# Layer 0's expert tiles 8 to 15 converted straight into weight slots, and the rows of s loaded together

## The chip, the cores and the metric

The kernel runs on one core of one Trainium2 chip. The time is that of the device for one execution, in microseconds; the median of several runs counts. The profile comes from one execution of its own, so its time differs a little from the median.

## The reference

Three stages follow each other, all in float32, on 4 batches, 8 heads, 576 positions, 512 model columns:

```
# attention, per batch and head
scores = (q @ k.T) / sqrt(64)
cum    = cumsum(maximum(s, 0))                       # s: (4, 8, 576)
scores = where(causal, -1e9, scores + minimum(-(cum[:, None] - cum[None, :]), 0))
attn   = softmax(scores);  x = attn @ v              # heads side by side: (4, 576, 512)
# layer 0
xn = (x - mean) / sqrt(var + 1e-6) * g_ln
x  = x + maximum(xn @ w_ch1, 0) @ w_ch2              # 512 -> 2048 -> 512
# layer 1: mixing over positions (U 576x32, V 32x576), then a second pair of 512 -> 2048 -> 512
u  = x + (x.T @ U @ V).T
out = u + maximum(u @ w_ch1', 0) @ w_ch2'
```

The weights arrive as float64 bit patterns and are turned into float32 on the chip.

## The kernel before, in words

**Tiles and steps.** The 2048 hidden columns are 16 tiles m of 128. Positions are cut into block A (the first 256) and block B (the other 320) of each batch. One *step* is one tile m on one block: `mlp1` multiplies by the tile's part of w_ch1, a relu follows, and `mlp2`, two steps later (`LAG`), multiplies by its part of w_ch2. Every product is done as three float32r matmuls on a high and a low part (lines 1364 to 1366 and 1397 to 1399). Layer 0 has 128 steps in this order: A0 and A1 (the block A of batches 0 and 1) on tiles 0 to 7 as steps 0 to 15, the same two on tiles 8 to 15 as steps 16 to 31, then A2 and A3 on tiles 8 to 15 and 0 to 7, then B0 to B3 one by one. Layer 1 has steps 128 to 207.

**Weight slots.** The pool `w` has 16 buffers of 512 KB: 8 tiles (`WSLOTS`), each with its half of w_ch1 (half 0) and of w_ch2 (half 1). When a later instance of a tile wants a slot, it takes that of the instance 8 before it, whose last use must be over. Tile n's first instance from 8 on has the slot of tile n - 8, which step n uses last.

**Conversion.** `f64_to_f32` takes a raw half tile (512 KB in a buffer of `wr`, of which there are four) with two ACT instructions (lines 517, 518) and one of DVE (line 520) into a PSUM bank; `split` then writes the high part (a copy on ACT or DVE, lines 374 or 375) and the low part (a subtraction on DVE, line 379).
- Tiles 0 to 7 (`fresh`) are split straight into their `w` slots (`w_split`) and the slot is also written to DRAM (`w_dr`, line 557), since later instances are read back from there (line 550).
- Tiles 8 to 15 go another way (`w_ahead`): raw load, conversion in place in `wr`, write to `w_dr` (line 566), and later a load into the slot. `W0` says over which steps these are laid.
- Layer 1's weights are converted ahead too (`w1_ahead`, `w2_ahead`), over the steps that `W1` gives.

**The front.** Before step 0, s is loaded. Four copies of its 32 rows stand on four groups of 32 partitions of `sc`, one load each, in two parts of columns (0 to 255, 256 to 575). relu and scaling (line 436), a running sum (line 438), its differences (line 451) and `ksum` (lines 457, 459) follow; the first matmul of the attention's scores reads `ksum` (line 761). A0's attention and its layer norm must be over before step 0.

**What sets the order.** Nothing is ordered by the program text. Each operation is given to a planner (`Plan`) with a priority, a cost, alternatives (ACT, DVE or POOL), and its reads and writes under keys; it places all of them on the engines by a list schedule, repeated `PASSES` times with due times from the schedule before. The emitted order of each engine, and of SP, which issues all DMAs, is the plan's. For the planner two operations that write the same key follow each other; the four row loads of one part have one key, `("s", c)`. Side work has positions in steps: `AT` (attention of each later block), `LN` (its layer norm), `W0`, `W1`. Where the plan leaves TensorE nothing to do before step 0, filler matmuls are put in (line 1552), which write a bank that nobody reads.

Of the kernel before, what the change touches and what calls it, by code (L numbers as in the profile page):

```python
# [31 lines left out]
LAST = ("C0", "C1", "C2", "C3", "T0")  # L32
W2SLOTS = 12

AT = {"A2": (3, 11), "A3": (6, 35), "B0": (24, 46), "B1": (48, 59), "B2": (67, 84), "B3": (78, 98)}
LN = {"A2": 15, "A3": 35, "B0": 59, "B1": 61, "B2": 84, "B3": 98}
W0 = (0, 8)
W1 = (10, 72, 50)
PASSES = 4


# [287 lines left out]
def mha_ffn_mixer_ffn(ctx: ExitStack, tc, qkv_p, qkv_a, qkv_b, s, g, w1, w2, U, V, out):  # L329
# [22 lines left out]
    def psum():  # L352
        return P.buf("ps", [128, 512])
# [15 lines left out]
    def load(prio, nbytes, fn, reads, writes, gate=None, rate=350.0):  # L369
        P.op(prio, {"sp": (475, fn)}, reads, writes, nbytes, gate, rate=rate)  # L370
# [13 lines left out]
    def split(prio, n, hi, lo, src, reads, wh, wl, psum=False, soft=0.0, slow=False):  # L384
        copy(prio, n, hi, src, reads, wh, psum, soft, slow)
        tt(prio, n, lo, src, lambda: f(hi()), ALU.subtract, list(reads) + list(wh), wl, psum, soft)
# [26 lines left out]
    def setup():  # L413
        sc, cum = P.buf("xc", [128, 1280]), P.buf("v", [128, 1280])
        late = 5
        part = ((0, 256, PRO), (256, S, late))

        for c, (c0, c1, pr) in enumerate(part):
            for y in range(4):
                load(pr, R * (c1 - c0) * 4, lambda y=y, c0=c0, c1=c1: nc.sync.dma_start(sc[R * y:R * (y + 1), c0:c1], s[:, c0:c1]), [], [(sc, ("s", c))])  # L420
        P.op(PRO, {"pool": (400, lambda: make_identity(nc, ident.tile))}, [], [ident])
        dve(PRO, 1, lambda: nc.vector.memset(eps.tile, 1e-6), [], [eps])
        dve(PRO, 1, lambda: nc.vector.memset(small.tile, 1e-9), [], [small])
        dve(PRO, 128, lambda: nc.vector.memset(ones.tile, 1.0 / DM), [], [ones], 0.521)
        P.op(PRO, {"pool": (600, lambda: nc.gpsimd.memset(causal.tile, 0.0))}, [], [causal])
        for y in range(4):
            act(PRO, R, lambda y=y: nc.scalar.activation(sel[R * y:R * (y + 1)], ident[R * y:R * (y + 1), R * y:R * (y + 1)], AF.Copy),
                [ident], [(sel, "y%d" % y)])

        def mask(d, n):  # L430
            return lambda: nc.gpsimd.affine_select(out=d, in_=d, compare_op=ALU.is_ge, fill=-8e9, base=0, pattern=[[-1, n]], channel_multiplier=1)

        P.op(PRO, {"pool": (266, mask(causal[:, 384:], 128))}, [causal], [causal])
        for c, (c0, c1, pr) in enumerate(part):
            k = (sc, ("s", c))
            dve(pr, c1 - c0, lambda c0=c0, c1=c1: nc.vector.tensor_scalar(out=sc[:, c0:c1], in0=sc[:, c0:c1], scalar1=0.0, scalar2=8.0, op0=ALU.max, op1=ALU.mult),
                [k], [k], 0.521)
            dve(pr, c1 - c0, lambda c0=c0, c1=c1: nc.vector.tensor_tensor_scan(
                cum[:, c0:c1], sc[:, c0:c1], sc[:, c0:c1], cum[:, c0 - 1:c0] if c0 else 0.0, ALU.add, ALU.max),
                [k] + [(cum, 0)] * c, [(cum, c)], 2.084)  # L440

        REL = {1: (sc, 576), 2: (sc, 832), 3: (sc, 0), 4: (cum, 640)}
        for i, (a, c) in REL.items():
            c0, c1 = COL[i], COL[i] + KEYS[i]
            pr = PRO if i == 1 else late
            key = [(a, ("s", y)) for y in range(2)] if i == 3 else [(a, 10 + i)]

            def rel(y0=0, y1=4, a=a, c=c, i=i):
                return a[R * y0:R * y1, c:c + KEYS[i]]

            dve(pr, KEYS[i], lambda i=i, rel=rel: nc.vector.tensor_scalar(
                out=rel(), in0=cum[:, :KEYS[i]], scalar1=cum[:, KEYS[i] - 1:KEYS[i]], scalar2=None, op0=ALU.subtract),
                [(cum, y) for y in range(1 + (i > 1))], key, 0.521, 128)
            if i == 4:
                load(pr, R * S * 4, lambda rel=rel: nc.sync.dma_start(cum_dr.tile, rel(0, 1)), key, [cum_dr])
                break
            act(pr, KEYS[i], lambda c0=c0, c1=c1, rel=rel: nc.scalar.activation(ksum[:, c0:c1], rel(), AF.Copy), key, [(ksum, i)])
            for y in (1, 3):
                dve(pr, KEYS[i], lambda y=y, c0=c0, c1=c1, rel=rel: nc.vector.tensor_tensor(
                    out=ksum[R * y:R * (y + 1), c0:c1], in0=rel(y, y + 1), in1=f(ksum[R * y:R * (y + 1), c0:c1]), op=ALU.subtract),  # L460
                    key + [(ksum, i)], [(ksum, i)])
        load(-1000, 2048, lambda: nc.sync.dma_start(g_sb.tile, g.rearrange("(k p) -> p k", p=128)), [], [g_sb])
        act(-1000, 4, lambda: nc.scalar.activation(g_sb.tile, g_sb.tile, AF.Copy, scale=-0.5), [g_sb], [g_sb])
# [38 lines left out]
    w_dr = {}  # L502
    for n, it in enumerate(inst):
        k = (it["l"], it["m"])
        it["fresh"] = k not in seen and n < WSLOTS
        if k not in seen:
            seen[k] = n
            w_dr[k] = P.fixed(dr_p.tile([128, 2, 2, 512], F32, name=f"w_dr{k[0]}_{k[1]}"))
    def f64_to_f32(prio, n, dst, raw, bd, br, words=(0, 1), psum=False):

        def pair(i):
            return raw().rearrange("p (c t) -> p c t", t=2)[:, :, i]

        def dv(fn, reads, writes):
            P.op(prio, {"dve": (68 + 1.042 * n, fn)}, reads, writes, port=not psum)

        act(prio, n, lambda: nc.scalar.activation(dst(), pair(1), AF.Prelu, scale=2.0 ** -112, alpha=-2.0 ** 32), [(br, words[1])], [bd], 135)
        act(prio, n, lambda: nc.scalar.activation(pair(0).bitcast(I32), pair(0).bitcast(U32), AF.Copy, scale=2.0 ** -29 * 0.9374),
            [(br, words[0])], [(br, words[0])], 135)
        dv(lambda: nc.vector.scalar_tensor_tensor(out=dst().bitcast(U32), in0=dst().bitcast(U32), scalar=3, in1=pair(0).bitcast(U32),  # L520
                                                  op0=ALU.logical_shift_left, op1=ALU.bitwise_or), [bd, (br, words[0])], [bd])

    def w_raw(prio, l, m, half, gate):
        raw = P.buf("wr", [128, 1024])

        def go():
            dst = raw.tile.bitcast(U32)
            if half == 0:
                nc.sync.dma_start(dst.rearrange("p (k c) -> p k c", k=KT), w1[l][m].bitcast(U32))
            else:  # L530
                nc.sync.dma_start(dst, w2[l][m * 128:(m + 1) * 128, :].bitcast(U32))

        load(prio, 128 * 4096, go, [], [raw], gate)
        return raw
# [8 lines left out]
    def w_split(n, half, gate):  # L543
# [11 lines left out]
        f64_to_f32(prio, 512, lambda: t.tile, lambda: raw.tile, t, raw, psum=True)  # L555
        split(prio, 512, lambda: w[:, 0], lambda: w[:, 1], lambda: t.tile, [t], [(w, 0)], [(w, 1)], psum=True)
        load(it["last"], 128 * 4096, lambda: nc.sync.dma_start(dr[:, half], f(w.tile)), [w], [(dr, half)])

    def w_ahead(n, half, gate):

        it = inst[n]
        prio, dr = it["first"] - 8, w_dr[it["l"], it["m"]]
        raw, t = w_raw(prio, it["l"], it["m"], half, gate), psum()
        f64_to_f32(prio, 512, lambda: t.tile, lambda: raw.tile, t, raw, psum=True)
        split(prio, 512, lambda: raw[:, :512].bitcast(F32R), lambda: raw[:, 512:].bitcast(F32R), lambda: t.tile, [t], [(raw, 0)], [(raw, 1)], psum=True)
        load(prio, 128 * 4096, lambda: nc.sync.dma_start(dr[:, half], raw.tile.rearrange("p (z c) -> p z c", z=2)), [raw], [(dr, half)])


    def w2_ahead(m, gate):
        prio = NS0 + m - 8  # L570
# [851 lines left out]
    def spread(items, a, b):  # L1422
        tot = sum(w for w, _ in items) or 1
        acc = 0.0
        for w, fn in items:
            put(a + (b - a - 0.25) * acc / tot, fn)
            acc += w

    halves = [(n, z) for n in range(len(inst)) for z in range(2)]

    def w_next(k, gate):
        if k < len(halves):
            w_load(*halves[k], gate)

    def w_step(k, gate):
        w_split(*halves[k], gate)
        w_next(k + 2, gate)

    for k, (n, z) in enumerate(halves):
        if n >= WSLOTS:  # L1440
            put(inst[n - WSLOTS]["last"] + LAG + 1 + 0.5 * z, lambda p, g, k=k: w_step(k, g))
    ahead = [(n, z) for n in range(WSLOTS, 2 * WSLOTS) for z in range(2)]
    for k, (n, z) in enumerate(ahead):
        if k >= 2:
            put(W0[0] + W0[1] * (k - 2) / 16, lambda p, g, n=n, z=z: w_ahead(n, z, g))
    for m in range(MT):
        at = W1[0] + W1[1] * m / 8 if m < 8 else W1[0] + W1[1] + W1[2] * (m - 8) / 8
        if m % 2 == 0:
# [76 lines left out]
    layer_norm_tok(4, 1)  # L1525
    for b in range(2):
        x_columns(10 + 8 * b, b)
    w_next(0, None)
    w_next(1, None)
    for k in range(2 * WSLOTS):  # L1530
        w_step(k, None)
    for n, z in ahead[:2]:
        w_ahead(n, z, None)

    def side(q):
        for pos, fn in plan.pop(q, []):
# [66 lines left out]
```

## Time and profile before

| | us |
|---|---|
| median of 3 runs | 1058.73 |
| lowest, highest | 1057.51, 1061.54 |
| the profiled execution | 1057.54 |
| its span | 1055.8 |
| granted TensorE clock, share of full speed | 0.999 |

PE is TensorE's matmuls, PEld its weight loads, DVE VectorE, ACT ScalarE, POOL GpSimd, SPq the DMA issues of SyncE. A line L550 is line 550 of the kernel. A matmul's busy time is modelled, and matmuls overlap each other; so sums of busy time by line can be longer than the stretch that they cover. Counts of records can be off by a few per cent. A wait is put down to what ended last.

### The profile page before, as it was taken

The page shows a single profiled execution, that of the slowest core. Times are in us where ns is not written, and L with a number is a line of the kernel's source. Part 1 is how long each engine was busy: PE and PEld are TensorE (multiplying, and loading weights), DVE is VectorE, ACT ScalarE, POOL GpSimd, SP SyncE. Part 2 cuts the span into 40 slices and gives each one's busy share as a digit, 9 for nine tenths or more (in the row PEclk, how much of TensorE's full clock was granted, in tenths as well). Part 3 has the DMA queues.
Part 4 walks back from the last instruction along what each step waited for, and adds up shares of the span by engine and source line. Part 5 has one row for each costly group of instructions (what it writes and reads, how often), then busy time and mean ns, then how long its engine had stood idle before and what let it go on. Part 6 is the DMA issues. An engine that isn't in the chain of part 4 may idle for free.

```text
span 1055.8 us, 20049 instructions
## 1 busy us (share of the span) xinstructions
PE 1038.2 (98%) x7469; PEld 967.0 (92%) x7469; DVE 676.2 (64%) x1709; ACT 490.1 (46%) x1152; POOL 150.8 (14%) x289
## 2 busy tenths in 40 slices
PE   9999999999999999999999999999999999999997
PEld 7799998899899999998999999898899999989997
DVE  6898777885897766787682526746455645744521
ACT  7978767774776566676552413412112211211211
POOL 0002123430541031323120001001000000100000
PEclk9999999999999999999999999999999999999999
DMA  9999999657833696487268799993663475276383
GB/s 310 343 325 347 365 325 308 189 164 283 269 126 133 235 351 202 136 291 269 68 232 331 241 337 367 341 365 116 222 232 135 135 268 186 94 259 206 121 279 100
DMA packets 100096, 253.55 MB, mean 240 GB/s; under 512 B 16512, under 2 KB 46464, under 8 KB 95648
## 3 DMA queue, kind: packets, MB, share of 16 engines
q1 hardware_dynamic: 100000, 252.28, 69.3%
q8 instruction: 59, 0.97, 0.4%
q14 instruction: 37, 0.30, 0.1%
HBM read 198.69 MB, written 62.99 MB: 248 GB/s over the span
## 4 chain that ended last, share of the span: by engine, by line
PE 78%; DVE 7%; DMA 6%; ACT 4%; issue 1%; SPq 0%; POOL 0%; DVEq 0%; ACTq 0%; POOLq 0%
PE ps L1364 6%; PE ps L1366 5%; PE ps L1365 5%; PE ps L1286 5%; PE ps L1288 5%; PE ps L1287 5%; PE acc L1397 4%; PE acc L1399 4%; PE acc L1398 4%; PE ps L862 3%; PE ps L820 3%; PE acc L1323 3%; PE acc L1324 3%; PE ps L1323 3%; PE ps L1324 3%; PE acc L1325 3%
## 5 line engine op out<-in xcount | busy, mean ns | idle before, releaser
L1364 PE MATMUL ps<-xh,w 128*128 128x256 f32 (+1 forms) x512 | 159.9, 312 | 1.0 <-DVE hl L1371 0.9
L1366 PE MATMUL ps<-xl,w 128*128 128x256 f32 (+1 forms) x512 | 151.3, 296 | 0.0
L1365 PE MATMUL ps<-xh,w 128*128 128x256 f32 (+1 forms) x512 | 151.3, 295 | 0.0
L1397 PE MATMUL acc<-hh,w 128*128 128x256 f32 (+1 forms) x448 | 136.2, 304 | 0.0
L1371 DVE SCALAR_TENSOR_TENSOR hl<-ps,hh 128x256 fp32r<-128x256 f32 (+1 forms) x144 | 64.7, 449 | 106.7 <-ACT hh L1370 105.7
L1399 PE MATMUL acc<-hl,w 128*128 128x256 f32 (+1 forms) x448 | 130.0, 290 | 0.1
L1398 PE MATMUL acc<-hh,w 128*128 128x256 f32 (+1 forms) x448 | 129.9, 290 | 0.0
L1370 ACT ACTIVATE hh<-ps 128x256 fp32r<-128x256 f32 (+1 forms) x144 | 58.0, 403 | 125.9 <-PE ps L1366 125.1
L1364 PEld LDWEIGHTS ps<-xh,w 128*128 128x128 f32 x512 | 97.0, 189 | 4.3 <-DVE hl L1371 1.1
L1365 PEld LDWEIGHTS ps<-xh,w 128*128 128x128 f32 x512 | 97.1, 190 | 0.6
L1246 ACT ACTIVATE w<-hl 128x256 fp32r<-128x256 f32 x88 | 36.0, 417 | 131.5 <-DVE hl L1266 131.5
L1366 PEld LDWEIGHTS ps<-xl,w 128*128 128x128 f32 x512 | 96.8, 189 | 0.0
L1397 PEld LDWEIGHTS acc<-hh,w 128*128 128x128 f32 x448 | 85.3, 190 | 3.5 <-issue 2.2
L1398 PEld LDWEIGHTS acc<-hh,w 128*128 128x128 f32 x448 | 85.3, 190 | 0.4
L1399 PEld LDWEIGHTS acc<-hl,w 128*128 128x128 f32 x448 | 85.1, 190 | 0.3 <-DVE hl L1371 0.3
L779 ACT ACTIVATE t<-t,mx 128x384 f32<-128x384 f32 (+4 forms) x112 | 68.9, 618 | 28.6 <-DVE mx L769 25.4
L1266 DVE TENSOR_TENSOR hl<-ps,hh 128x256 f32<-128x256 f32 x128 | 48.6, 419 | 47.9 <-PE ps L1288 46.8
L1266 DVE TENSOR_TENSOR hh<-ps,hh 128x256 f32<-128x256 f32 x64 | 27.1, 423 | 76.1 <-ACT hh L374 74.8
L379 DVE TENSOR_TENSOR pB<-ps,pB 128x512 fp32r<-128x512 f32 (+1 forms) x112 | 62.4, 571 | 16.3 <-ACT pB L374 15.6
L374 ACT ACTIVATE pB<-ps 128x512 fp32r<-128x512 f32 (+3 forms) x119 | 59.1, 502 | 25.5 <-PE ps L820 25.2
L820 PE MATMUL ps<-ident,t 128*128 128x128 f32 x400 | 64.8, 276 | 4.6 <-POOL wr L381 1.4
L374 ACT ACTIVATE hh<-ps 128x256 f32<-128x256 f32 x31 | 11.9, 384 | 109.7 <-PE ps L1288 109.6
(249 smaller groups left out, 2825.0 us busy)
## 6 DMA issues: line engine op xcount, KB each, us to landing
w<-w_dr SPq DMA_DIRECT2D x128, 512.0 KB, 7.5
pB<-w_dr SPq DMA_DIRECT2D x34, 1024.0 KB, 5.3
w_dr<-wr SPq DMA_DIRECT2D x48, 512.0 KB, 5.5
qk<-w_dr SPq DMA_DIRECT2D x26, 768.0 KB, 5.6
wr<-w1a SPq DMA_DIRECT2D x16, 512.0 KB, 5.9
wr<-w2a SPq DMA_DIRECT2D x16, 512.0 KB, 6.1
w_dr<-w SPq DMA_DIRECT2D x16, 512.0 KB, 6.8
wr<-w1b SPq DMA_DIRECT2D x16, 512.0 KB, 7.2
```

Of the source, the lines that this page charges most:

```text
L374: "act": ((51 if psum else 94) + 0.8333 * n, lambda: nc.scalar.activation(out(), a(), AF.Copy)),
L779: act(prio, K, lambda t=t, mx=mx, o=o, K=K, x=x, y=nt * z + x: nc.scalar.activation(t[:, o:o + K], t[:, o:o + K], AF.Exp, bias=mx[:, (1 if ...
L820: nc.tensor.transpose(ps[:, 128 * j:128 * (j + 1)], t[:, c:c + 128], ident.tile)
L1266: dve(st - 1000, 256, lambda: nc.vector.tensor_tensor(out=d.tile, in0=region(r), in1=a.tile, op=ALU.add), [p, a], [d])
L1323: nc.tensor.matmul(aa[z].tile, w[:, 0, sl], h[:, 0], start=first, stop=False)
L1364: nc.tensor.matmul(ps[:, :n], lhs(k, 0), xh[:, k, :n], start=k == 0, stop=False)
L1365: nc.tensor.matmul(ps[:, :n], lhs(k, 1), xh[:, k, :n], start=False, stop=False)
L1366: nc.tensor.matmul(ps[:, :n], lhs(k, 0), xl[:, k, :n], start=False, stop=k == KT - 1)
L1371: dve(st - 1000, n, lambda: nc.vector.scalar_tensor_tensor(out=hl[:, :n], in0=ps[:, :n], scalar=0.0, in1=f(hh[:, :n]), op0=ALU.max, op1=AL ...
L1397: nc.tensor.matmul(a, w[:, 0, sl], hh[:, :n], start=new, stop=False)
L1398: nc.tensor.matmul(a, w[:, 1, sl], hh[:, :n], start=False, stop=False)
L1399: nc.tensor.matmul(a, w[:, 0, sl], hl[:, :n], start=False, stop=last and (z == 1 or blk == "B"))
```

## The change

Five edits go together.
- The four row loads of s have a key of their own each, so that for the planner none of them follows another; those who read the rows name all four keys.
- Tiles 8 to 15 are `fresh` as well. `w_ahead` is gone. Their raw loads go through `w_next`, and `w_split` converts them straight into their `w` slots, laid one position behind the last use of the slot (instead of three for those that are read back); the slot is then written to DRAM as those of tiles 0 to 7 are.
- Raw loads are issued three half tiles ahead instead of two.
- `AT`, `LN` and `W1` have other values. `W0` has too, but nothing reads it any more.
- `it16` is only another name for the flag `fresh`.

```diff
-AT = {"A2": (3, 11), "A3": (6, 35), "B0": (24, 46), "B1": (48, 59), "B2": (67, 84), "B3": (78, 98)}
-LN = {"A2": 15, "A3": 35, "B0": 59, "B1": 61, "B2": 84, "B3": 98}
-W0 = (0, 8)
-W1 = (10, 72, 50)
+AT = {"A2": (1, 13), "A3": (1, 34), "B0": (28, 48), "B1": (48, 61), "B2": (67, 84), "B3": (78, 98)}
+LN = {"A2": 17, "A3": 34, "B0": 61, "B1": 61, "B2": 84, "B3": 98}
+W0 = (1, 14)
+W1 = (16, 66, 53)
...
-                load(pr, R * (c1 - c0) * 4, lambda y=y, c0=c0, c1=c1: nc.sync.dma_start(sc[R * y:R * (y + 1), c0:c1], s[:, c0:c1]), [], [(sc, ("s", c))])
+                load(pr, R * (c1 - c0) * 4, lambda y=y, c0=c0, c1=c1: nc.sync.dma_start(sc[R * y:R * (y + 1), c0:c1], s[:, c0:c1]), [], [(sc, ("s", c, y))])
...
-            k = (sc, ("s", c))
+            k = [(sc, ("s", c, y)) for y in range(4)]
...
-        it["fresh"] = k not in seen and n < WSLOTS
+        it["fresh"] = k not in seen
...
-    def w_ahead(n, half, gate):
-
-        it = inst[n]
-        prio, dr = it["first"] - 8, w_dr[it["l"], it["m"]]
-        raw, t = w_raw(prio, it["l"], it["m"], half, gate), psum()
-        f64_to_f32(prio, 512, lambda: t.tile, lambda: raw.tile, t, raw, psum=True)
-        split(prio, 512, lambda: raw[:, :512].bitcast(F32R), lambda: raw[:, 512:].bitcast(F32R), lambda: t.tile, [t], [(raw, 0)], [(raw, 1)], psum=True)
-        load(prio, 128 * 4096, lambda: nc.sync.dma_start(dr[:, half], raw.tile.rearrange("p (z c) -> p z c", z=2)), [raw], [(dr, half)])
...
     def w_step(k, gate):
         w_split(*halves[k], gate)
-        w_next(k + 2, gate)
+        w_next(k + 3, gate)
 
     for k, (n, z) in enumerate(halves):
         if n >= WSLOTS:
-            put(inst[n - WSLOTS]["last"] + LAG + 1 + 0.5 * z, lambda p, g, k=k: w_step(k, g))
-    ahead = [(n, z) for n in range(WSLOTS, 2 * WSLOTS) for z in range(2)]
-    for k, (n, z) in enumerate(ahead):
-        if k >= 2:
-            put(W0[0] + W0[1] * (k - 2) / 16, lambda p, g, n=n, z=z: w_ahead(n, z, g))
+            put(inst[n - WSLOTS]["last"] + (1.0 if it16(n) else LAG + 1) + 0.5 * z, lambda p, g, k=k: w_step(k, g))
...
-    w_next(0, None)
-    w_next(1, None)
+    for k in range(3):
+        w_next(k, None)
     for k in range(2 * WSLOTS):
         w_step(k, None)
-    for n, z in ahead[:2]:
-        w_ahead(n, z, None)
```

## Rows read from the trace of the kernel before

**Rows 1.** The page's head and part 1: busy time, share, instructions.

```profile
span 1055.8 us, 20049 instructions
PE 1038.2 (98%) x7469; PEld 967.0 (92%) x7469; DVE 676.2 (64%) x1709; ACT 490.1 (46%) x1152; POOL 150.8 (14%) x289
```

**Rows 2.** Windows: stretch, length, busy of each engine, clock, DMA share, GB/s.

```profile
0.00:22.10 22.10, 20.10 (x166) 17.08 (x166) 12.87 (x24) 15.41 (x29) 1.72 (x10) 1.00 0.90 315
22.10:51.20 29.10, 27.59 (x234) 21.81 (x235) 25.59 (x98) 27.40 (x65) 0.41 (x2) 1.00 0.95 334
51.20:82.00 30.80, 30.48 (x272) 29.12 (x271) 27.76 (x93) 24.91 (x68) 3.21 (x6) 1.00 0.96 326
...
82.00:149.00 67.00, 66.20 (x574) 63.76 (x573) 56.38 (x155) 49.50 (x140) 11.88 (x24) 1.00 0.99 355
...
51.20:560.00 508.80, 501.04 (x3857) 473.75 (x3856) 397.09 (x1021) 341.28 (x825) 127.73 (x262) 1.00 0.73 245
```

**Rows 3.** Windows of line 1552 (fillers): PE busy, PEld busy, clock, DMA.

```profile
0.00:22.10 22.10, 20.10 (x166) 17.08 (x166) 1.00 0.90 315
22.10:51.20 29.10, 5.74 (x39) 3.73 (x39) 1.00 0.95 334
```

**Rows 4.** Timeline of the front: start, length, engine, line, operation, what the wait ended.

```profile
0.75 0.40 SPq L420 DMA_DIRECT2D xc<-s  x1
...
12.43 0.42 SPq L420 DMA_DIRECT2D xc<-s  x1
...
18.70 0.29 DVE L436 TENSOR_SCALAR xc<-xc 128x256 f32<-128x256 f32 x1
...
22.14 0.78 PE L761 MATMUL ps<-ksum,sel 64*128 64x128 f32 x2 [0.91 <-DVE ksum L459]
...
51.25 0.36 PE L1364 MATMUL ps<-xh,w 128*128 128x256 f32 x1
```

**Rows 5.** Line 420, the eight row loads of s: time from issue to landing.

```profile
DMA to landing us min/median/max: 1.7/6.0/6.6
```

**Rows 6.** Groups by line, 0 to 51.2 us: busy, mean ns, idle before.

```profile
L520 DVE SCALAR_TENSOR_TENSOR ps<-ps,wr 128x512 uint32<-128x512 uint32 x15 | 10.4, 693 | 8.4 <-ACT wr L518 8.4
L379 DVE TENSOR_TENSOR w<-ps,w 128x512 fp32r<-128x512 f32 x15 | 10.2, 683 | 0.2
...
L518 ACT ACTIVATE wr<-wr 128x512 int32<-128x512 uint32 x17 | 11.3, 672 | 0.8 <-DMA wr<-w2a 0.7
L517 ACT ACTIVATE ps<-wr 128x512 f32<-128x512 f32 x16 | 10.2, 636 | 4.7 <-DMA wr<-w1a 4.6
...
L374 ACT ACTIVATE w<-ps 128x512 fp32r<-128x512 f32 x12 | 7.0, 591 | 0.6 <-DVE ps L520 0.6
```

**Rows 7.** Waits of ACT and DVE, 0 to 22.1 us: in total, times, longest.

```profile
ACT ps L517 <- DMA wr<-w1a: 4.6, 3, 1.9
...
DVE ps L520 <- ACT wr L518: 8.2, 5, 5.1
```

**Rows 8.** Windows of line 520 (one per conversion): DVE busy and count.

```profile
51.20:82.00 30.80, 4.13 (x6) 1.00 0.96 326
82.00:113.00 31.00, 5.46 (x8) 1.00 0.98 352
113.00:149.00 36.00, 2.06 (x3) 1.00 0.99 358
```

**Rows 9.** Window of line 1364 (four in each step): PE and PEld busy, counts.

```profile
51.20:82.00 30.80, 9.02 (x30) 5.70 (x30) 1.00 0.96 326
```

**Rows 10.** Waits of TensorE, 51.2 to 560 us, the four longest.

```profile
PE ps L820 <- POOL wr L381: 1.4, 1, 1.4
PE ps L962 <- DVE ls L379: 1.1, 1, 1.1
PE ps L820 <- DVE mx L748: 0.9, 1, 0.9
PE ps L1364 <- DVE hl L1371: 0.9, 1, 0.9
```

**Rows 11.** Instructions on w_dr: issue ns min/median/max, first and last start, count.

```profile
L550 SPq DMA_DIRECT2D w<-w_dr x96: 319/422/1725, 101.3 to 627.7; - x96
...
L566 SPq DMA_DIRECT2D w_dr<-wr x16: 319/374/806, 60.1 to 139.2; - x16
```

More of the change, by code (lines that the diff above doesn't have):

```diff
@@ L434, in setup @@
         for c, (c0, c1, pr) in enumerate(part):
-            k = (sc, ("s", c))
+            k = [(sc, ("s", c, y)) for y in range(4)]
             dve(pr, c1 - c0, lambda c0=c0, c1=c1: nc.vector.tensor_scalar(out=sc[:, c0:c1], in0=sc[:, c0:c1], scalar1=0.0, scalar2=8.0, op0=ALU.max, op1=ALU.mult),
-                [k], [k], 0.521)
+                k, k, 0.521)
             dve(pr, c1 - c0, lambda c0=c0, c1=c1: nc.vector.tensor_tensor_scan(
                 cum[:, c0:c1], sc[:, c0:c1], sc[:, c0:c1], cum[:, c0 - 1:c0] if c0 else 0.0, ALU.add, ALU.max),
-                [k] + [(cum, 0)] * c, [(cum, c)], 2.084)
+                k + [(cum, 0)] * c, [(cum, c)], 2.084)
         REL = {1: (sc, 576), 2: (sc, 832), 3: (sc, 0), 4: (cum, 640)}
@@ L445, in setup @@
             pr = PRO if i == 1 else late
-            key = [(a, ("s", y)) for y in range(2)] if i == 3 else [(a, 10 + i)]
+            key = [(a, ("s", c, y)) for c in range(2) for y in range(4)] if i == 3 else [(a, 10 + i)]
             def rel(y0=0, y1=4, a=a, c=c, i=i):
@@ L1427, in spread, with it16 @@
             acc += w
+    def it16(n):
+        return inst[n]["fresh"]
     halves = [(n, z) for n in range(len(inst)) for z in range(2)]
```

## The prediction

> **What bounds the kernel now.** I read the page first: TensorE (PE) is busy 1038.2 us of a span of 1055.8 [rows 1]. The reader should see there that little can be gained by feeding TensorE better on average, and ask where the missing time lies. The busy time by stretch answers it [rows 2]. From step 0 (the first expert matmul, at 51.25 us [rows 4]) to 560 us TensorE is idle 508.80 - 501.04 = 7.8 us in all, and its longest single wait there is 1.4 us [rows 10]. Ahead of step 0 it is different. The filler matmuls of line 1552, which compute nothing, fill 20.10 us of the first 22.1 us and 5.74 us of the next 29.1 [rows 3]. TensorE is idle 22.10 - 20.10 = 2.0 us and 29.10 - 27.59 = 1.5 us there. Of the 51.2 us ahead of step 0, then, 20.10 + 5.74 + 2.0 + 1.5 = 29.3 us do no work and 21.9 us do. That front is the only large loss.
>
> What ends last in the front is read from the timeline [rows 4]. The four row loads of s (first part) go out between 0.75 and 12.43 us, other loads between them; the last lands some 6.0 us after its issue [rows 5], VectorE (DVE) begins on s at 18.70, and the first useful matmul, which reads ksum, starts at 22.14. From s landed to that matmul is 22.14 - 18.70 = 3.4 us. Behind 22.14 the front is held by ACT and DVE, not by TensorE: ACT is busy 27.40 and DVE 25.59 of 29.10 us [rows 2]. They share their time there between A0's attention and the conversion of layer 0's tiles. The DMA engines are 0.90 to 0.99 busy up to 149 us [rows 2].
>
> **The change, part by part.** *The four row loads.* They were chained in the planner only; now they can go out one behind another. The last is then issued at about 0.75 + 3 x 0.45 = 2.1 us (an estimate from the spacing that their issue cost of 0.40 to 0.42 us allows [rows 4]) and lands 1.7 to 6.6 us later (the smallest and the largest of the eight [rows 5]), at 3.8 to 8.7. With 3.4 us behind it the first useful matmul comes at 7.2 to 12.1 instead of 22.14, that is 10 to 15 us earlier. I take the median landing of 6.0: 11.5, so 10.6 us earlier. The weight loads go out up to three issues (1.3 us) later for it, which delays the first conversion by as much.
>
> *What of it reaches step 0.* Below: everything that now stands ahead of step 0 still does. Then only idle time of the busier engine can go. ACT is busy 15.41 + 27.40 = 42.8 of 51.2 us and idle 8.4. Of these some 2.7 stay (0.75 before anything starts and one wait of 1.9 for the first weights [rows 7]); so at most 5.7, and with the 1.3 us delay about 4. Above: conversions move behind step 0. By 51.2 DVE has done 15 of the 16 conversions of tiles 0 to 7 [rows 6], though step 0 wants two and each later step two more. One costs ACT 0.64 + 0.67 + 0.59 = 1.9 us and DVE 0.69 + 0.68 = 1.4 us [rows 6]. Five put off free 9.5 us of ACT, and the whole 10 to 15 us can come through. I take 9 us, nearer to the upper end, because of the 31 us behind step 0, next point.
>
> *Tiles 8 to 15 straight into slots.* Now six conversions (five of them into wr) run between 51.2 and 82 us [rows 8], where step 7 is half done (30 of line 1364's matmuls, four a step [rows 9]). In the new form no tile from 8 on can be split before a slot is free, which is after step 8. So about five conversions, 9.5 us of ACT and 7 of DVE, leave the stretch behind step 0, and that is the room for five of tiles 0 to 7. They go into 82 to 149, which holds eleven now [rows 8]: DVE from 56.38 to 63.4 of 67 us (95%), ACT from 49.50 to 59.0 (88%) [rows 2]. It fits only because A2's and A3's attention starts at position 1 instead of 3 and 6 and so takes work out again. The conversions themselves are neither more nor fewer. What is late next here is the split into the slot: it stands in ACT's and DVE's queues, behind it are the relu of the running step and the exponentials, and TensorE waits for those. Today's waits of TensorE on DVE and POOL of 0.9 to 1.4 us [rows 10] bound one such stall; none to ten of them, 0 to 12 us. I take one, 1.4 us.
>
> *The round trip.* Sixteen loads of 512 KB (line 550, of 96 [rows 11]) go; the write behind the conversion stays, from w instead of wr. At 355 GB/s [rows 2] these 8.4 MB are 24 us of DMA time, most of them off the stretch 82 to 149 that is 0.99 busy. No wait of TensorE there is on these loads [rows 10], so their direct worth is nothing, at the most the 0.8 us that TensorE idles from 82 to 149 (67.00 - 66.20). They also leave SP's queue, where they stand between the loads of q, k and v. I count 0. Without this relief the earlier start would have run into full DMA engines.
>
> *Third raw load ahead, new intervals.* One more raw load in flight of four wr buffers: ACT's 4.6 us of waits for w1a in the front [rows 7] are the most that it gives, and these are in the bound above. W1 starts at 16 instead of 10 and ends at 135 instead of 132; layer 1's first tile is wanted at step 128, its last at 143. Behind 149 us the same work is dealt out anew: it can at best give back the 7.8 us of idle [rows 2] less what lies before, and lose as much; I take 0, and -3 to +5 for the range.
>
> *Sum.* -9.0 + 1.4 = -7.6. The profiled run took 1057.54 us (span 1055.8 and 1.7 around it), 1.2 below the median of 1058.73. That makes 1049.9 from the one and 1051.1 from the other; I say 1050.5.
>
> One rule speaks for more. The Trainium skill (Perfetto Trace Analysis, Identifying the Most-Contended Engine) says that matmul busy time is no measure of how near TensorE is to its limit and that the share of weight loads is. Loads are busy 473.75 us from 51.2 to 560 us [rows 2], which would leave 35.1 us of room instead of 7.8. The waits of TensorE there, 1.4 us at the longest [rows 10], don't bear that out; it is rival 4.
>
> **Rivals.** *1, deeper front* (like the forecast, but all of the 10 to 15 us arrives and no split stalls): 1058 - 13 = 1045. For it: the DMA relief and the five deferred conversions. Against: DVE at 95% behind it. *2, the gain stays in the front* (rows queued behind weight loads, or step 0 still behind all 15 conversions): only ACT's 4 us come, less 1.4: 1056. For it: a row load behind weight loads took 6.0 us and more, against 1.7 at best [rows 5], and the order on SP is a planner's. That is also the case in which the change doesn't do what it says. By the Trainium skill (DMA: Bandwidth & Descriptors, Queues, rings and completion order) each DMA engine consumes descriptors in ring order, so a row behind a 512 KB load would wait for it; the spread from 1.7 to 6.6 agrees. *3, slower:* the conversions of tiles 8 to 15 come late into their slots. Each tile has from step n-8 to step n, about 31 us; if DVE (95% by the count above) lags, each of eight tiles costs TensorE a wait of 1.4 us (11 us), and DVE's arrears, 5 conversions x 1.4 = 7 us, are passed on too. With 4 us from the front: 1058 + 14 = 1072; it decides from where stalls and arrears together exceed the front's gain: against 9 us, from four stalls and half the arrears (5.6 + 3.5 us). For it: DVE's share; against: reading back needed the same conversions about 12 us earlier. *4, more room on TensorE:* half of 35.1 us goes, 1033.
>
> **How the numbers follow.** Forecast 0.42 (1047 to 1053.4), rival 1 0.16, rival 2 0.28, rival 3 0.12, rival 4 0.02. About 0.5%, 5.3 us, is what a measurement can tell from no change: faster is below 1053.4, slower above 1064.0. So faster 0.42 + 0.16 + 0.02 = 0.60, the same 0.28, slower 0.12. The range takes in rival 2 and most of rival 1: 1043 to 1061, and leaves out rivals 3 and 4 and the end of 1.
>
> **What would show it.** Right: four issues of line 420 back to back near 1 us; the first matmul of line 761 at 8 to 13 us; step 0 near 42; fewer than 205 fillers (I expect about 130); the first conversion into w of tile 8 behind step 8; loads of line 550 down to 80; a DMA share below 0.95 from 100 to 149. Wrong: step 0 at 47 or later (rival 2), or waits on the split lines 375 and 379 in front of step 16 to 24 (rival 3). If step 0 is 9 us earlier and the end is not, the time was given back between 149 and 560 us, and idle time of TensorE there must have grown from 7.8.

## The result and the profile after

The changed kernel takes 1050.39 us (median of 5, 1046.47 to 1052.06), the kernel before 1058.73 (1056.74 to 1061.54): ratio 0.9917, 95% interval 0.9890 to 0.9945. The forecast was 1050.5. The profiled execution after took 1051.12 us.

The page's head and part 1, and the windows of TensorE and the other engines (stretch, length, busy PE, PEld, DVE, ACT, POOL, clock, DMA share, GB/s) answer to [rows 1, 2]. Step 0 now starts at 39.84 us, so the first cut stands at 39.6.

```profile
span 1049.3 us, 19869 instructions
PE 1028.1 (98%) x7377; PEld 958.3 (91%) x7377; DVE 667.0 (64%) x1686; ACT 496.4 (47%) x1165; POOL 154.2 (15%) x299
```

```profile
0.00:39.60 39.60, 35.73 (x294) 28.66 (x294) 30.06 (x109) 30.19 (x71) 2.13 (x12) 1.00 0.86 296
39.60:560.00 520.40, 511.64 (x3928) 484.81 (x3929) 396.73 (x1014) 360.31 (x860) 131.99 (x272) 1.00 0.70 238
560.00:1049.30 489.30, 480.74 (x3157) 444.85 (x3155) 240.25 (x564) 105.94 (x235) 20.13 (x15) 1.00 0.64 224
...
39.60:82.00 42.40, 41.29 (x357) 39.10 (x358) 36.50 (x110) 33.43 (x86) 3.50 (x8) 1.00 0.92 324
82.00:149.00 67.00, 64.39 (x547) 61.83 (x546) 53.28 (x134) 53.69 (x137) 11.80 (x22) 1.00 0.96 331
```

The fillers' windows after (line 1539 now) answer to [rows 3]; the group of them counts 113, where it was 205.

```profile
0.00:22.10 22.10, 9.08 (x64) 7.08 (x64) 1.00 0.73 236
22.10:39.60 17.50, 6.68 (x49) 4.79 (x49) 1.00 1.01 372
```

The timeline of the front after answers to [rows 4]: the four rows go out together, VectorE starts on s at 4.04 instead of 18.70, the first useful matmul at 8.34 instead of 22.14, step 0 at 39.84 instead of 51.25.

```profile
0.75 1.80 SPq L420 DMA_DIRECT2D xc<-s  x4
...
4.04 0.29 DVE L436 TENSOR_SCALAR xc<-xc 128x256 f32<-128x256 f32 x1 [2.96 <-DMA xc<-s]
...
8.34 0.33 PE L751 MATMUL ps<-ksum,sel 64*128 64x128 f32 x2
...
39.84 0.36 PE L1354 MATMUL ps<-xh,w 128*128 128x256 f32 x1 [0.51 <-DVE xl L1036]
```

The ledger is the most useful reading. The span is filler + idle time of TensorE + the rest of its busy time (useful). Before: 25.8 + 17.6 + 1012.4. After: 15.8 + 21.2 + 1012.3. The useful time is the same to 0.1 us, for 7264 matmuls without the fillers in either, so all that moved is filler (-10.0) and idle time (+3.6). By place: ahead of step 0, filler and idle went from 29.3 to 15.76 + 39.60 - 35.73 = 19.6 us, 9.7 less. From step 0 to 560 us idle rose from 7.8 to 520.40 - 511.64 = 8.8. From 560 us to the end it rose from 6.3 (17.6 less the 3.5 ahead of step 0 and the 7.8 behind it) to 489.30 - 480.74 = 8.6. The spans of the profiled pair differ by 6.5 us; the medians lie 8.3 apart.

TensorE's longest waits after (in total, times, longest) answer to [rows 10]; the whole execution is shown, and only one of them is longer than the longest of before in layer 0. The two on `pB<-w_dr` lie in layer 1.

```profile
PE ps L751 <- DVE mx L759: 1.6, 1, 1.6
PE ps L1354 <- DMA pB<-w_dr: 1.6, 2, 1.3
PE ps L810 <- POOL wr L381: 1.3, 1, 1.3
PE ps L810 <- POOL t L787: 1.2, 1, 1.2
```

The instructions on w_dr answer to [rows 11]: the loads into slots are 80, not 96, and begin at 230 us, not at 101; the writes from slots are 32 (16 before).

```profile
L550 SPq DMA_DIRECT2D w<-w_dr x80: 319/430/1467, 230.3 to 620.4; - x80
...
L557 SPq DMA_DIRECT2D w_dr<-w x32: 326/570/1608, 20.0 to 152.7; - x32
```

### The profile page after: what moved, and what is told of

Its sections match the earlier page's. It is cut to its first block, busy times and chain, and to the rows that moved or that the text cites. A ratio compares the mean times of both kernels' runs of the same rounds, so it can differ in the third digit from the quotient of the medians.

```text
span 1049.3 us, 19869 instructions
## 1 busy us (share of the span) xinstructions
PE 1028.1 (98%) x7377; PEld 958.3 (91%) x7377; DVE 667.0 (64%) x1686; ACT 496.4 (47%) x1165; POOL 154.2 (15%) x299
## 4 chain that ended last, share of the span: by engine, by line
PE 75%; DMA 14%; DVE 4%; ACT 2%; issue 2%; SPq 1%; POOL 1%; DVEq 0%; POOLq 0%; ACTq 0%
PE ps L1354 6%; PE ps L1355 5%; PE ps L1356 5%; PE ps L1276 5%; PE ps L1278 5%; PE ps L1277 5%; PE acc L1387 4%; PE acc L1388 4%; PE acc L1389 4%; PE ps L852 3%; PE acc L1313 3%; PE acc L1314 3%; PE ps L1313 3%; PE ps L1314 3%; PE ps L1315 3%; PE acc L1315 3%
## 5 line engine op out<-in xcount | busy, mean ns | idle before, releaser
L379 DVE TENSOR_TENSOR pB<-ps,pB 128x384 fp32r<-128x384 f32 (+1 forms) x112 | 62.0, 571 | 14.8 <-ACT pB L374 14.0
L374 ACT ACTIVATE pB<-ps 128x384 fp32r<-128x384 f32 (+3 forms) x115 | 56.5, 504 | 23.6 <-PE ps L810 22.9
```

The costliest lines, as they stand in the source:

```text
L374: "act": ((51 if psum else 94) + 0.8333 * n, lambda: nc.scalar.activation(out(), a(), AF.Copy)),
```

## The experiments

Each was timed in alternation with the kernel before (whose medians were 1057.6 to 1058.95) and profiled once. The table is the ledger of the profiled executions, worked out as above from the page's head, part 1 and the fillers' group; time and ratio are of the timed runs. One execution can lie some us off its median (two raw loads ahead: 1057.29 against 1053.10; late writes: 1049.33 against 1052.65), so differences of 3 us between two rows of the ledger tell little. All kernels have the same 7264 useful matmuls.

| kernel | median us | ratio to before (95%) | filler | idle | useful |
|---|---|---|---|---|---|
| before | 1058.73 | | 25.8 | 17.6 | 1012.4 |
| the change | 1050.39 | 0.9917 (0.9890 to 0.9945) | 15.8 | 21.2 | 1012.3 |
| rows only | 1063.14 | 1.0060 (1.0047 to 1.0072) | 16.9 | 29.6 | 1014.3 |
| rows only, new intervals | 1067.77 | 1.0085 (1.0065 to 1.0104) | 14.4 | 29.3 | 1023.4 |
| direct only | 1069.12 | 1.0113 (1.0097 to 1.0129) | 26.4 | 25.0 | 1015.7 |
| direct only, old intervals | 1063.97 | 1.0046 (1.0029 to 1.0063) | 26.9 | 19.7 | 1014.0 |
| new intervals only | 1070.29 | 1.0106 (1.0082 to 1.0129) | 26.7 | 24.8 | 1015.1 |
| change, old intervals | 1051.93 | 0.9953 (0.9940 to 0.9965) | 17.0 | 21.2 | 1012.2 |
| change, W1 half a step later | 1056.81 | 0.9973 (0.9956 to 0.9990) | 14.3 | 26.1 | 1016.6 |
| change, two raw loads ahead | 1053.10 | 0.9951 (0.9932 to 0.9969) | 15.4 | 24.3 | 1015.6 |
| change, late writes | 1052.65 | 0.9930 (0.9907 to 0.9953) | 15.3 | 21.0 | 1011.2 |
| change, extra copies in 80 to 165 | 1067.27 | 1.0105 (1.0084 to 1.0125) | 16.3 | 32.7 | 1015.6 |
| change, extra copies in 140 to 700 | 1058.99 | 1.0011 (0.9991 to 1.0031) | 16.1 | 26.1 | 1013.7 |

My theory was that the early rows make the gain and direct conversion keeps it. The rivals were that one of the two, or the intervals, does it alone.

**Rows only.** The kernel before with the keys of the change:

```diff
-..., [], [(sc, ("s", c))])
+..., [], [(sc, ("s", c, y))])
...
-            k = (sc, ("s", c))
+            k = [(sc, ("s", c, y)) for y in range(4)]
```

> The kernel before with the row keys alone: tiles 8 to 15 still make the round trip, intervals as before. Its emitted order holds 113 fillers, as many as the changed kernel. Theory (the rows give the front, direct conversion only keeps it): first useful matmul near 8.3 us, step 0 near 40, some 9.5 us less of filler and idle in the front, but the DMA engines are full (0.95 and more) from 50 to 140 and ACT and DVE have the early conversions again, so 2 to 4 us come back as idle time of TensorE: 1051 to 1054. Rival A (the rows are the whole change): 1050.4 plus or minus 1.5. Rival B (without direct conversion the front's gain is lost): 1056 to 1060.

It took 1063.14: slower than before, and beyond what even rival B had. The front is that of the changed kernel (113 fillers, the first step at 40.6 us), so the 9 us are there, and are lost with interest behind it. TensorE's waits from 100 to 180 us, and windows of this kernel:

```profile
PE acc L1397 <- DMA w<-w_dr: 5.8, 3, 2.7
PE ps L1364 <- DMA w<-w_dr: 2.3, 1, 2.3
```

```profile
130.00:150.00 20.00, 12.71 (x95) 11.94 (x96) 10.51 (x30) 8.08 (x23) 3.74 (x7) 0.91 1.01 372
82.00:180.00 98.00, 87.29 (x718) 82.92 (x717) 74.99 (x208) 64.87 (x177) 21.62 (x44) 0.97 0.96 335
```

The reader is to see a DMA share of 1.01 where TensorE is busy only 12.71 of 20 us, and that it waits for the very loads that the round trip needs. One can be followed: the write of a converted half goes out at 131.4 us and lands at 141.6, a load from w_dr goes out at 141.7 and lands at 148.6, and TensorE goes on at 148.7. The DMA engines were as full before (0.99 from 82 to 149 us [rows 2]) without such waits; what is new is that the steps come 10 us earlier, and the read-back tiles are too late for them.

**Rows only, with the new intervals.** A second plan for the same question; the diff is the one above and the constants of the change.

> The kernel before with the new row keys and with AT, LN, W0 and W1 of the changed kernel; tiles 8 to 15 still make the round trip. A second plan for the rows alone. If the round trip on full DMA engines is what turned the early rows into a loss, this one loses as well, with TensorE waiting on w<-w_dr for 5 us or more between 100 and 180 us: 1058 to 1068. If that run was an unlucky plan, or the old intervals were at fault: 1050 to 1055.

1067.77, with waits of TensorE on `w<-w_dr` of 3.8 + 0.8 us between 100 and 180 us, a little under the 5 expected. So a second plan with the rows alone is no faster than the kernel before either. But the new intervals by themselves take 1070.29 (below), and against that the rows cost nothing: 2.5 us less, with spreads that overlap (1066.02 to 1070.51 and 1065.64 to 1074.48). That they are a loss by themselves is shown on the old intervals alone.

**Direct conversion only.** The changed kernel with the old row keys (the diff above, reversed):

> The changed kernel with the old row keys: direct conversion, third load ahead and new intervals, but the rows chained in the planner. Its order holds 209 fillers (before: 205). Theory: the front stays at some 29 us of filler and idle, step 0 at 49 to 52; what is left is worth 0 to 2 us: 1056.5 to 1059.5. Rival A: 1058.7. Rival B (direct conversion is worth something of its own): 1052 to 1055.

> Direct conversion and third load ahead with the old row keys, as in the run with direct conversion only, but with AT, LN and W1 of the kernel before. That run took 1069, 11 over the kernel before, with the same front. If its loss came from the new intervals, which suit a front that is 10 us shorter, this one comes to 1056 to 1061. If direct conversion itself costs something without the early rows, it stays at 1064 to 1070. By the share of DMA alone it should be 1055 to 1058.

1069.12 with the new intervals, ten above what the theory gave, and 1063.97 with the old ones. Against the new intervals alone (1070.29) direct conversion loses nothing; on the old ones it loses 5 us, against what the DMA share let me expect. Line 520's windows (one per conversion) in the kernel with the old intervals, and all engines there in two stretches:

```profile
51.20:60.00 8.80, 2.77 (x4) 1.00 1.02 349
60.00:82.00 22.00, 0.00 (x0) 1.00 0.65 237
82.00:113.00 31.00, 3.46 (x5) 1.00 0.67 234
113.00:149.00 36.00, 4.81 (x7) 1.00 0.94 317
```

```profile
60.00:82.00 22.00, 21.61 (x183) 20.77 (x184) 16.25 (x48) 8.93 (x22) 1.47 (x1) 1.00 0.65 237
140.00:160.00 20.00, 17.89 (x134) 16.42 (x133) 18.88 (x48) 19.39 (x54) 6.90 (x14) 0.91 0.99 366
```

From 60.0 to 96.8 us nothing is converted, and of the 22 us shown ACT is busy 8.93. Tiles 0 to 7 are done and no slot is free before step 8. Before, five conversions into wr filled that hole [rows 8]. They come back between 82 and 180, and from 140 to 160 DVE and ACT are 94% and 97% busy, TensorE idles 2.1 us and its granted clock is 0.91 in the mean. So direct conversion by itself takes away freedom. With the early rows there is other work for a part of the hole, the conversions of tiles 0 to 7: with the change, ten conversions start between 41.2 and 62.5 us (seven of tiles 0 to 7, three of the raw halves behind them), and the hole lasts only from 63.2 to 88.3. That this is what the early rows do for direct conversion is read from the windows; no run tests it by itself.

**Intervals.** The changed kernel with the old AT, LN and W1, and the kernel before with the new ones and the new W0, which it does read (the conversions of tiles 8 to 15 are then laid over 14 steps instead of 8):

> The changed kernel with AT, LN and W1 of the kernel before. Theory: the front is the same (some 113 fillers), the stretches behind it are dealt out differently and lose or gain up to 3 us: 1048 to 1054. Rival C (the new intervals carry the gain): 1056 or more, with TensorE's idle time between 40 and 560 us at 15 us instead of 8.8.

> The kernel before with AT, LN, W0 and W1 of the changed kernel, nothing else. If the intervals carry gain of their own: 1053 or less. By the mechanism, nothing but a new plan with the front at some 205 fillers: 1056 to 1064.

1051.93 and 1070.29. The intervals alone don't carry the gain; on the old mechanism they cost 11.4 us, more than I had expected. How much of that is W0 is open.

With these runs both parts can be compared within one set of intervals. Old intervals: rows +4.4 us, direct conversion +5.2, both -6.8. New intervals: -2.5, -1.2, -19.9. In either set both together are some 16 us better than the sum of the two alone.

**How much is the plan.** Half a step in W1, and two raw loads ahead instead of three:

```diff
-W1 = (16, 66, 53)
+W1 = (16.5, 66, 53)
...
-        w_next(k + 3, gate)
+        w_next(k + 2, gate)
```

> The changed kernel with W1 at (16.5, 66, 53) instead of (16, 66, 53), half a step: nothing of the mechanism is touched, but the planner lays out everything anew. It measures how much of a time is the particular plan. Theory (the mechanism decides): 1048 to 1053. Rival E (the gain is luck of one plan): 1055 or more.

> The changed kernel with raw loads two half tiles ahead, as before, instead of three. If the third load in flight matters, ACT and DVE wait longer for raw weights in the front and behind it (now 0.6 to 1.4 us in each wait), and the time is 1054 to 1060; if it doesn't, it is a new plan and nothing more: 1049 to 1057, with the front at 110 to 120 fillers.

1056.81 and 1053.10. Half a step costs 6.4 us of the 8.3, which by the number is rival E's side. Its front is as short (14.3 us of filler), so the front's gain is no luck; how much of it is given back is: TensorE's idle time from 180 to 560 us is 9.8 us, with the change 4.3. No such small step was tried on the kernel before, so how far its own time is that of a lucky or unlucky plan isn't known. The third load shows no worth that could be told from that.

**DMA bytes put back.** The changed kernel, with a copy of 512 KB from DRAM to DRAM behind each write of tiles 8 to 15. The order of PE, DVE, ACT and POOL is the same, so the plan is not at play:

```diff
+        def store():
+            nc.sync.dma_start(dr[:, half], f(w.tile))
+            if n >= WSLOTS:
+                nc.sync.dma_start(spare[2 * (n - WSLOTS) + half].tile, w1[0][m].bitcast(U32))
```

> The changed kernel with a 512 KB copy from DRAM to DRAM issued on SP right behind each of the 16 writes of tiles 8 to 15 to w_dr; the order of PE, DVE, ACT and POOL is the same as that of the changed kernel, and the copies feed nothing. This puts back the bytes that the round trip's loads took, and 16 issues. Theory (the DMA relief by itself is worth nothing directly, since TensorE waited for none of these loads): within 1.5 us of the changed kernel, 1049 to 1052. Rival D (the relief is what keeps the gain): 2 to 5 us slower, 1053 to 1056, with waits of TensorE, ACT and DVE on loads of q, k, v between 80 and 180 us.

1067.27: 17 us, more than any side had expected. Windows, and ACT's waits from 82 to 180 us:

```profile
82.00:149.00 67.00, 57.93 (x480) 54.90 (x478) 44.85 (x112) 45.22 (x116) 10.80 (x19) 1.00 1.00 365
149.00:180.00 31.00, 26.27 (x199) 24.45 (x200) 21.48 (x65) 20.68 (x59) 5.01 (x11) 0.89 0.74 281
```

```profile
ACT qk L374 <- DMA qk<-qkvA: 8.6, 4, 3.2
ACT ps L517 <- DMA wr<-w2b: 6.7, 1, 6.7
ACT ps L517 <- DMA wr<-w1a: 3.4, 2, 2.9
```

With the DMA share at 1.00 instead of 0.96, q and k come late; ACT, whose order is fixed, waits for them, and TensorE idles 9.1 us in the first of these stretches (2.6 with the change) and 4.7 in the second (0.7). Since both traces hold the same matmuls in the same order, the start of one and the same matmul can be compared: the one at 94.7 us of the change is 1.8 us later here, the one at 166.6 us 16.7 later, and one near the end, at 1040 us, 15.1 later. So all is lost where the copies lie (issued from 79.9 to 165.4 us). Two limits of this run: the planner had not reckoned with the copies, so a plan that does may lose less; and a copy also writes DRAM, which the round trip's loads did not.

**The same bytes elsewhere.** The copies stand behind the writes of layer 1's w2 tiles:

> The changed kernel with the same 16 copies of 512 KB from DRAM to DRAM as in the run with extra copies, but behind the writes of layer 1's w2 tiles, which lie between 140 and 700 us; the order of PE, DVE, ACT and POOL is again that of the changed kernel. If it is the full DMA engines between 80 and 150 us that made the extra copies cost 17 us, then here, where the DMA share is 0.6, they cost 0 to 3 us: 1050 to 1053.5. Rival F (16 more transfers and issues cost that much anywhere, by their bytes or by SP's time): 1060 or more.

1058.99, 8.6 us above the change: half, not nothing. Neither side was right. The windows with the change, then with these copies:

```profile
149.00:180.00 31.00, 30.28 (x254) 28.13 (x254) 25.76 (x77) 23.78 (x69) 10.71 (x24) 1.00 0.57 186
560.00:700.00 140.00, 139.14 (x928) 132.86 (x927) 68.35 (x146) 42.84 (x89) 6.58 (x5) 1.00 0.89 321
```

```profile
149.00:180.00 31.00, 28.58 (x232) 25.93 (x232) 24.05 (x70) 21.79 (x63) 10.49 (x22) 1.00 0.58 209
560.00:700.00 140.00, 137.24 (x907) 131.44 (x905) 66.28 (x140) 42.94 (x89) 6.57 (x5) 0.99 0.89 323
```

TensorE idles 2.4 instead of 0.7 us in the first and 2.8 instead of 0.9 in the second. The loss is not spread evenly over the 16 copies. By the start of the same matmul, this kernel is 0.8 us ahead at 149.6 us of the change and 1.8 behind at 166.6; at 491.5, after seven more copies, it is 0.2 behind; then 3.1 at 556.8, 6.4 at 624.4, and 6.7 near the end. So a transfer and its issue on SP have no fixed price here: the seven copies issued between 208 and 458 us cost nothing that could be told. The cost arises in three places, one of them a stretch in which the DMA share of the change is only 0.59 (488 to 558 us). There ACT waits 4.5 us for a raw load (`wr<-w2b`), in an order that was made without the copies.

**Bytes taken out.** The writes of tiles 8 to 15 put off to 8 steps before the slot's last use:

```diff
+            if it16(n):
+                put(inst[n]["last"] - 8 + 0.5 * z, lambda p, g, n=n, z=z: w_store(n, z, g))
```

> The changed kernel with the writes of tiles 8 to 15 from their slots to w_dr put off to 8 steps before the slot's last use (about 175 to 215 us) instead of right behind the conversion (80 to 153 us). This takes another 8.4 MB out of the stretch where the DMA engines are 0.96 busy and puts it where they are 0.57 to 0.75. Theory with the DMA engines as the limit of that stretch: TensorE's idle time from 82 to 149 falls from 2.6 us to about 1, 0 to 3 us faster: 1047 to 1050.5. Rival (after the change the DMA engines no longer limit): 1050.4 plus or minus 2, as for any new plan.

1052.65 (1049.06 to 1055.40). From 82 to 149 us the DMA share fell from 0.96 to 0.71, but TensorE idled 3.7 us there, not less:

```profile
82.00:149.00 67.00, 63.30 (x537) 60.70 (x536) 54.96 (x137) 52.78 (x138) 12.27 (x24) 1.00 0.71 236
```

The time is nearer to the rival (1050.4 plus or minus 2) than to the theory: taking more bytes out gains nothing that could be told, and there is no sign that the DMA engines still limit the changed kernel. The run can't exclude 1 to 3 us, since it is a new plan, and since the same stretch differs between executions of one order (TensorE idles 2.6 us from 82 to 149 us with the change, 1.0 with the late copies, which begin at 142). No version tried has a lower median than the change.

## Why the prediction was right, step by step

**The rows.** Right in mechanism, the landing too pessimistic: I took the median of 6.0 us behind other loads. First in the queue they landed sooner (the four that matter, those of the first part, 1.7 to 1.8 us after their issue), and VectorE began at 4.04. Line 420, 0 to 5 us:

```profile
DMA to landing us min/median/max: 1.7/1.7/1.8
```

The first useful matmul came 13.8 us earlier; my bounds were 10 to 15, my value 10.6. The delay of the weights was too small by far: their first load went out at 4.96 us instead of 1.21, since loads of q, k and v (line 626) stand ahead of it too, and the first conversion ran at 16.3 us instead of 6.2. I had put 1.3 us for it.

**What reaches step 0.** I took 9 us. Step 0 came 11.4 us earlier, and filler and idle ahead of it shrank by 9.7; the difference is useful work (21.9 us ahead of step 0 before, 20.0 after) that now runs behind it. Line 520's windows after answer to [rows 6, 8]:

```profile
0.00:39.60 39.60, 6.21 (x9) 1.00 0.86 296
39.60:60.00 20.40, 4.91 (x8) 1.00 0.90 308
60.00:74.00 14.00, 2.02 (x3) 1.00 0.95 374
74.00:82.00 8.00, 0.00 (x0) 1.00 0.91 275
```

Only 9 conversions are done ahead of step 0, where 15 were. (One that runs across 60 us counts in both windows.) That is the upper of my two cases, for the reason given, and it alone: ACT is busy 30.19 us ahead of step 0 instead of 42.8, and its idle time there, 9.4 us, did not shrink (8.4 before). The 4 us of idle time in my lower case did not come.

**Tiles 8 to 15.** The hole until step 8 came as described, and deferred conversions fill it in part, until 63.2 us; the first half of tile 8 is split at 77.6, just behind step 8. Direct conversion alone shows the hole without that filling. My load for 82 to 149 us was wrong: DVE is busy 53.28 us there, not 63.4, and ACT 53.69, not 59.0, although 18 conversions run there and not 16. The attention that I had said would leave the stretch did leave (16 exponentials of line 769 instead of 20 before), but I had taken nothing off for it. The stalls, +1.4 in the forecast, were 1.0 from step 0 to 560 us. That the size fits is luck: no wait of TensorE from 74 to 180 us is on a split into a slot; the longest there, 1.2 us, is on `t` from POOL.

**The round trip.** Here the forecast failed in a part that the total hides. I counted its direct worth as nothing, since TensorE waited for none of these loads before. Putting the bytes back into the finished plan costs 17 us, all in the stretch from which the change took them. What I wrote beside it, that the earlier start would have run into full DMA engines, was the point: on the old intervals rows alone go from 1058 to 1063, and with direct conversion to 1052. The DMA share from 100 to 149 us, which I expected below 0.95, is 0.98 (1.00 before): the earlier work took the place of the loads.

**Behind 560 us.** I counted 0; idle time grew by 2.2 us, of which waits for `pB<-w_dr` are 1.4 (2.1 us in all, 0.7 before).

**How sure the right number is.** Five plans with both parts (the change, old intervals, W1 shifted, two loads ahead, late writes) lie from 1050.4 to 1056.8; the four with one part from 1063 to 1069; the two with neither at 1058.7 and 1070.3. That the two parts gain only together is shown on these eleven plans, and for the rows alone read in the waits. Of the rivals, the second falls with step 0 at 39.84 us, the third with the waits above, and the fourth with the useful time, which stayed at 1012 us. That the gain is 8 us rather than 3 is this plan's, and that the forecast of 1050.5 met the median to 0.1 us is luck: the front gave 9.7 instead of 9, the rest took 3.2 instead of 1.4, and the profiled pair and the medians differ by 1.8.

## What to carry to other kernels

When two edits free and load the same resource, price them together: here each alone lost 4 to 5 us on the old intervals and won nothing on the new ones, and both together gained 7 and 20 us against the same intervals without them. A resource that nobody waits for is not free if it is 0.96 busy and the change pulls work forward into it; ask what its share will be after the shift, and which loads the engines will then wait for. And where a planner lays out everything anew, time a few plans that differ in nothing that matters before a difference of 6 us is given a cause.

## What the runs showed of the hardware that was not expected

In two executions stalls of TensorE cost twice, as idle time and as a lower clock behind them. In rows only, TensorE was busy 6.53 of 10 us from 130 to 140 us, and in the following 20 us the mean granted clock was 0.83 of full speed, a mix of its two levels of 2.4 and 1.2 GHz:

```profile
130.00:140.00 10.00, 6.53 (x59) 6.14 (x60) 6.61 (x22) 6.43 (x20) 3.74 (x7) 1.00 1.02 388
140.00:150.00 10.00, 6.17 (x38) 5.79 (x37) 3.90 (x8) 1.64 (x4) 0.00 (x0) 0.83 0.99 357
150.00:160.00 10.00, 8.24 (x56) 7.95 (x55) 4.50 (x14) 3.00 (x9) 1.03 (x3) 0.83 0.91 314
```

The useful busy time, 1012.4 us before, was 1014.3 in that execution and 1023.4 in rows only with the new intervals, where the clock was 0.80 from 149 to 180 us: the same matmuls, 2 to 11 us longer. Such a plan loses more than its idle time shows. The clock doesn't account for every longer useful time: with W1 half a step later it is 1016.6 us at a mean clock of 0.998 over the whole execution, where the change has 1012.3 at 0.997; why is open.
